# Recurrent states of a decayed attention: kept block-diagonal as they leave PSUM, in place of copies into zeroed tiles

## Chip, core and metric

One NeuronCore of a Trainium2 chip. The kernel is a single launch. The metric is the time of the slowest core in microseconds of the device, here of the only one. Lower is better.

## What is computed

The reference is a linear attention with decay, followed by two matmuls with a leaky activation between them. Inputs: q, k, v of (4 batches, 8 heads, 768 positions, 64), a decay `lam` per head, and weights `w_in` (512x2048), `w_out` (2048x512), `alpha` (2048).

```python
for b in range(nb):                      # blocks of 64 positions
    intra = einsum('bhic,bhjc->bhij', qb, kb) * Dmask
    intra = einsum('bhij,bhjd->bhid', intra, vb)
    inter = einsum('bhid,bhde->bhie', qb * lam_pow, kv_state)
    out[:, :, sl] = intra + inter
    kv_state = lam_block * kv_state + einsum('bhsd,bhse->bhde', kb * rev_pow, vb)
x = out.transpose(0, 2, 1, 3).reshape(3072, 512)
h = x @ w_in
return (maximum(h, 0) + alpha * minimum(h, 0)) @ w_out
```

The state `kv_state` is a 64x64 matrix for each batch and head. It carries everything that earlier blocks contribute to later ones.

## The kernel before

The kernel works with blocks of L = 128 positions, in pairs (W = 256), so there are three pairs of blocks, pb = 0, 1, 2, in each batch. A *unit* is one block pair of one batch and one half of the heads (four heads, `hh` = 0 or 1): 24 units, numbered in the list `units`. Two batches make a *column* c of 512 positions; six columns pass through the two weight matrices.

For each unit: q and k are cast to fp16 (`cast`), transposed on PE or by DMA (`transposes`, `transposed`), k is weighted with its decay (`key_decayed`), the transposed q too (`decayed`). `score_products` makes the scores with 64x64 tiles of PE, `masked` multiplies them with the decay mask on DVE. `state_products` (L432) makes the products of k and v with 64x64 tiles, one for each head, sixteen for each block. `inter` (L371) applies the states to the queries with full 128x128 matmuls that take two heads at once. So its weights must be a 128x128 matrix with the states of the two heads on the diagonal and zeros beside it.

Before the change there are two sets of tiles for the states. `R[b, hh, n]` holds the state behind block n - 1, dense: 128 partitions (two heads of 64), two head pairs, 64 columns. `RD[b, hh]` holds the two block-diagonal weights of the current pair. `zero_states` writes zeros into RD once on DVE; later only the diagonal is written. `states` (L459) does that. For the first pair (pb = 0) ACT copies the products of block 0 from PSUM into R (L486), and in two halves of 64 partitions into the diagonal of RD (L481); DVE adds the decayed state to the products of block 1 (`dense`, L469: one instruction for each head pair). For later pairs DVE runs `dense` for each block and POOL copies R into the diagonal of RD, four copies of 64 partitions for a unit (L495). The order of the two on ACT is set by the argument `first`.

`cluster(old, new)` (L497) puts two units together in one tile `acc` of two PSUM banks, one for each block: columns 0 to 255 of a bank hold the outputs of the old unit, 256 to 383 the state products of the new one. Every call takes a fresh tile from a pool with one buffer, so it begins when all that read the former tile are done. `state(n, pair)` (L518) makes the state products of a unit by themselves, in two other banks; it is called for units 1, 2, 3 and 6. `up` (L528) is the product with `w_in`, then ACT (L541) and DVE (L550) make the activation g; `down` and `down_last` are the product with `w_out`, and `store` brings the sums out through ACT. `fill` issues matmuls whose result nobody reads.

The order on every engine is written out by hand: a list of calls from L634 to L946 up to the third column, and behind it `attention_steps` and `weave`, which mix the steps of one column's attention with the matmuls of others. Each engine takes its instructions in the order of the calls and waits on semaphores. Loads of k, q and v are issued on SP, those of the weights on POOL (`load_win` L98, `load_wout` L110), and their places are in the same list. The start of the list, the calls for units 0 to 3, ends with the first `up`:

```python
cluster(None, 0, "A", "V")
...
state(1, "hh", "V")
...
cluster(0, None, "A")
...
cluster(1, None, "A")
state(2, "hh", "A")
...
cluster(2, None, "A")
scores(3)
...
state(3, "to", "A")
cluster(3, None, "V")
```

Of the kernel before, what the change touches and what calls it, by code (L numbers as in the profile page):

```python
# [11 lines left out]
def kernel(  # L12
# [52 lines left out]
    def load_alpha():  # L65
        nc.sync.dma_start(out=alpha_sb, in_=moe_alpha.rearrange("(t p) -> t p", p=128))

    R = {
        (b, hh, n): const.tile([128, 2, D], fp16, name=f"R{b}_{hh}_{n}")
        for b in range(B)  # L70
        for hh in range(2)
        for n in range(1, S // L)
    }
    RD = {
        (b, hh): const.tile([128, 2, 2, 2, D], fp16, name=f"RD{b}_{hh}")
        for b in range(B)
        for hh in range(2)
    }
# [3 lines left out]
    def load(c, bi, x, half=None):  # L82
# [6 lines left out]
        nc.sync.dma_start(  # L89
            out=raws[c, bi][i][:, heads, :],  # L90
            in_=(k, q, v)[i][b, heads, ds(pb * W, W), :].rearrange("h (p e) d -> p h (e d)", e=2),
        )
# [30 lines left out]
    def zero_states(batches, eng="V"):  # L123
        for b in batches:
            for hh in (1, 0):
                if eng == "G":
                    nc.gpsimd.memset(RD[b, hh].bitcast(int32), 0)
                else:
                    nc.vector.memset(RD[b, hh], 0.0)

    zero_states((1, 0))
# [25 lines left out]
    fill(4, "h", RD[1, 1].rearrange("p a e h d -> p (a e h d)"))  # L157
# [213 lines left out]
    def inter(n, ot):  # L371
        co, bo, ho = units[n]
        pbo, bb = co // 2, 2 * (co % 2) + bo
        for a in range(2):
            if 2 * pbo + a == 0:
                continue
            for hp in range(2):
                nc.tensor.matmul(  # L378
                    ot[a][:, hp, :].rearrange("p (e j) -> p e j", e=2),
                    lhsT=RD[bb, ho][:, a, hp].rearrange("p h d -> p (h d)"),  # L380
                    rhs=T[n]["qdT"][:, :, hp, ds(a * 64, 64)],
                    start=(hp == 0),
                    stop=False,
                    skip_group_check=True,
                )
# [26 lines left out]
    def intra(n, ot):  # L412
# [19 lines left out]
    def state_products(n, kv, fresh):  # L432
        t = T[n]
        for hp in range(2):
            for e in range(2):
                for hl in range(2):
                    for a in blocks_of(n):
                        p = ds(a * 64, 64)
                        nc.tensor.matmul(  # L439
                            kv[a][ds(hl * 64, 64), hp, :],  # L440
                            lhsT=t["kdec"][p, e, 2 * hp + hl, :],
                            rhs=t["v16"][p, 2 * hp + hl, e, :],
                            start=(fresh and hp == 0 and e == 0),
                            stop=(e == 1),
                            skip_group_check=True,
                        )

    def attended(n, acc, eng):
# [10 lines left out]
    def states(n, kv, first="A"):  # L459
# [18 lines left out]
        def diagonal():  # L478
            for hl in range(2):
                p = ds(hl * 64, 64)  # L480
                nc.scalar.activation(RD[b, hh][p, 1, :, hl, :], kv[0][p], AF.Copy)  # L481

        if pb == 0:
            if first == "A":
                diagonal()
            nc.scalar.activation(R[b, hh, 1], kv[0], AF.Copy)  # L486
            if first != "A":
                diagonal()
            dense()
            return  # L490
        dense()
        for a in range(2):
            for hl in range(2):
                p = ds(hl * 64, 64)
                nc.gpsimd.tensor_copy(out=RD[b, hh][p, a, :, hl, :], in_=R[b, hh, 2 * pb + a][p])  # L495

    def cluster(old, new, eng="A", first="A"):  # L497

        acc, ot, kv = accumulators()
        if old is not None:  # L500
            inter(old, ot)
        if new is not None:
            score_products(new)
        if old is not None:
            intra(old, ot)
        if new is not None:
            state_products(new, kv, old is None)
            masked(new)
        if old is not None:
            attended(old, acc, eng)  # L510
        if new is not None:
            states(new, kv, first)
# [5 lines left out]
    def state(n, pair, first="A"):  # L518
# [125 lines left out]
    zero_states((2,), "V")  # L644
# [30 lines left out]
    cluster(None, 0, "A", "V")  # L675
# [14 lines left out]
    state(1, "hh", "V")  # L690
# [11 lines left out]
    state(2, "hh", "A")  # L702
# [11 lines left out]
    state(3, "to", "A")  # L714
# [47 lines left out]
    zero_states((3,), "V")  # L762
    cast(7, "k16", "A")
    down(0, 0, 1, 4, "op")
    cluster(None, 4, "A", "V")
# [15 lines left out]
    cluster(5, 7, "A", "V")  # L781
# [27 lines left out]
    state(6, "hh", "A")  # L809
# [179 lines left out]
```

## Time and profile before

| what | value |
|---|---|
| median of 3 runs | 215.39 us (215.36 to 215.66) |
| the profiled execution | 215.25 us, its span 213.2 us |
| PE busy | 204.6 us (96%), 2084 matmuls |
| DVE busy | 135.4 us (64%) |
| ACT busy | 117.7 us (55%) |
| POOL busy | 79.8 us (37%) |
| chain that ended last | PE 91%, ACT 3%, DMA 2% |
| granted clock of PE | 0.998 |

The profile shows one execution. "Busy" is the share of time in which an engine has an instruction at work. PE is the matmul engine, DVE the vector engine, ACT the scalar engine, POOL the general one, SP only issues DMAs. Rows of a group give the line, engine, operation, output and inputs, shapes and count, then the busy time, the mean of one in ns, and the idle time before them with what ended it. Rows of the timeline give the start and the length in us. The chain of waits goes back from the last instruction to what released each step. The line numbers are those of the kernel before.

### The profile page before, as it was taken

The page shows a single profiled execution, that of the slowest core. Times are in us where ns is not written, and L with a number is a line of the kernel's source. Part 1 is how long each engine was busy: PE and PEld are TensorE (multiplying, and loading weights), DVE is VectorE, ACT ScalarE, POOL GpSimd, SP SyncE. Part 2 cuts the span into 40 slices and gives each one's busy share as a digit, 9 for nine tenths or more (in the row PEclk, how much of TensorE's full clock was granted, in tenths as well). Part 3 has the DMA queues.
Part 4 walks back from the last instruction along what each step waited for, and adds up shares of the span by engine and source line. Part 5 has one row for each costly group of instructions (what it writes and reads, how often), then busy time and mean ns, then how long its engine had stood idle before and what let it go on. Part 6 is the DMA issues. An engine that isn't in the chain of part 4 may idle for free.

```text
span 213.2 us, 5185 instructions
## 1 busy us (share of the span) xinstructions
PE 204.6 (96%) x2084; PEld 105.9 (50%) x2084; DVE 135.4 (64%) x247; ACT 117.7 (55%) x225; POOL 79.8 (37%) x148
## 2 busy tenths in 40 slices
PE   7677999999999999999999999999999999999994
PEld 2354444555545465455554554554554444444453
DVE  6795788767899877979965655555546344444000
ACT  7987766577685537366654644644534543444121
POOL 3597002425446664336688358348301000000000
PEclk9999999999999999999999999999999999999999
DMA  6999999998968599996929996044011001110212
GB/s 165 290 274 205 207 205 288 251 300 255 283 158 234 107 173 277 229 242 187 233 46 263 222 246 167 0 101 98 0 52 49 33 20 51 49 49 3 98 49 98
DMA packets 60603, 33.37 MB, mean 157 GB/s; under 512 B 16276, under 2 KB 57636, under 8 KB 60580
## 3 DMA queue, kind: packets, MB, share of 16 engines
q1 hardware_dynamic: 56340, 28.85, 55.3%
q0 software_dynamic: 4224, 4.19, 11.9%
q8 instruction: 16, 0.26, 0.5%
q14 instruction: 7, 0.06, 0.1%
q10 hardware_dynamic: 16, 0.00, 0.0%
HBM read 27.27 MB, written 6.29 MB: 157 GB/s over the span
## 4 chain that ended last, share of the span: by engine, by line
PE 91%; ACT 3%; DMA 2%; POOL 1%; DVE 1%; issue 0%; ACTq 0%; POOLq 0%
PE h_ps L533 39%; PE o_ps L563 33%; PE o_ps L586 7%; PE s L394 4%; PE acc L419 2%; DMA kraw<-in_k_dram 2%; PE acc L378 2%; PE acc L439 1%; PE tp L321 1%; POOL kdec L293 1%; ACT qkT L252 1%; ACT RD L481 1%; DVE sm L405 1%; PE unread L148 1%; ACT qk L252 1%; PE tpx L341 1%
## 5 line engine op out<-in xcount | busy, mean ns | idle before, releaser
L550 DVE SCALAR_TENSOR_TENSOR g<-m,oma,h_ps 128x512 f16<-128x512 f32 (+1 forms) x98 | 71.1, 736 | 50.2 <-ACT m L541 48.3
L533 PE MATMUL h_ps<-xT,w_in_sb 128*128 128x512 f16 (+1 forms) x392 | 92.9, 375 | 0.0
L541 ACT ACTIVATE m<-h_ps 128x512 f32<-128x512 f32 (+1 forms) x98 | 57.4, 588 | 56.6 <-PE h_ps L533 56.4
L563 PE MATMUL o_ps<-w_out_sb,g 128*128 128x512 f16 x320 | 80.2, 380 | 0.0
L533 PEld LDWEIGHTS <-w_in_sb 128*128 128x128 f16 x392 | 37.9, 98 | 43.1 <-issue 0.2
L563 PEld LDWEIGHTS <-g 128*128 128x128 f16 x320 | 29.8, 98 | 33.5
L495 POOL COPY RD<-R 64x128 f16<-64x128 f16 x64 | 19.7, 309 | 43.0 <-DVE R L469 39.5
L405 DVE TENSOR_TENSOR sm<-s,dmask 128x1024 f16<-128x1024 f32 x24 | 29.3, 1221 | 4.0 <-PE s L394 3.9
L576 ACT ACTIVATE o_sb<-o_ps 128x512 f32<-128x512 f32 (+2 forms) x26 | 14.7, 564 | 20.1 <-PE o_ps L586 10.9
L293 POOL TENSOR_TENSOR kdec<-kraw,kdecay 128x512 f16<-128x512 f32 x18 | 19.2, 1072 | 5.4 <-DMA kraw<-in_k_dram 5.0
L252 ACT ACTIVATE xT<-acc 128x512 f16<-128x512 f32 x22 | 13.1, 598 | 10.5 <-PE acc L439 8.8
L355 POOL TENSOR_TENSOR qdT<-qkT,qdecay 128x512 f16<-128x512 f16 (+1 forms) x15 | 15.5, 1036 | 2.9 <-ACT qdecay L237 2.2
L586 PE MATMUL o_ps<-w_out_sb,g 128*128 128x512 f16 (+2 forms) x96 | 14.1, 308 | 0.0
L469 DVE SCALAR_TENSOR_TENSOR R<-R,rdecay,acc 128x64 f16<-128x64 f16 x56 | 12.4, 276 | 0.9 <-ACT R L486 0.5
L256 POOL CAST qk<-kraw 128x512 f16<-128x512 f32 x14 | 8.5, 610 | 11.9 <-DMA kraw<-in_k_dram 6.8
L586 PEld LDWEIGHTS <-g 128*128 128x128 f16 x96 | 8.1, 98 | 6.1
L394 PE MATMUL s<-qkT 64*64 64x128 f16 x384 | 10.0, 221 | 0.9 <-DVE qkT L254 0.4
L256 POOL CAST v<-vraw 128x512 f16<-128x512 f32 x15 | 9.3, 621 | 3.4 <-DMA vraw<-in_v_dram 2.4
L252 ACT ACTIVATE qk<-qraw 128x512 f16<-128x512 f32 x17 | 10.4, 623 | 0.0
L419 PE MATMUL acc<-sm,v 64*64 64x128 f16 x384 | 9.6, 218 | 0.1
L378 PE MATMUL acc<-qdT,RD 128*128 128x128 f16 x80 | 8.4, 219 | 0.9 <-ACT RD L481 0.8
L378 PEld LDWEIGHTS <-RD 128*128 128x128 f16 x80 | 6.2, 98 | 6.0 <-ACT RD L481 1.1
(66 smaller groups left out, 116.8 us busy)
## 6 DMA issues: line engine op xcount, KB each, us to landing
out_dram<-o_sb SPq DMA_DIRECT2D x23, 256.0 KB, 2.3
kraw<-in_k_dram SPq DMA_DIRECT2D x18, 256.0 KB, 6.5
vraw<-in_v_dram SPq DMA_DIRECT2D x14, 256.0 KB, 5.7
qraw<-in_q_dram SPq DMA_DIRECT2D x7, 512.0 KB, 5.9
qraw<-in_q_dram SPq DMA_DIRECT2D x10, 256.0 KB, 5.4
vraw<-in_v_dram SPq DMA_DIRECT2D x5, 512.0 KB, 5.9
w_in_sb<-in_moe_w_in_dram POOLq DMA_DIRECT2D x4, 512.0 KB, 8.6
w_out_sb<-in_moe_w_out_dram POOLq DMA_DIRECT2D x4, 512.0 KB, 12.7
```

The costliest lines, as they stand in the source:

```text
L252: nc.scalar.activation(out, in_, AF.Copy)
L256: nc.gpsimd.tensor_copy(out=out, in_=in_)
L293: engine(eng).tensor_tensor(out=kdec, in0=kr, in1=kdecay[:, ds(4 * hh, 4), :].rearrange("p h e -> p e h").unsqueeze(3).to_broadcast([128, ...
L378: nc.tensor.matmul(ot[a][:, hp, :].rearrange("p (e j) -> p e j", e=2), lhsT=RD[bb, ho][:, a, hp].rearrange("p h d -> p (h d)"), rhs=T[n][" ...
L394: nc.tensor.matmul(t["s"][ds(a * 64, 64), hl, hp, 1 - e, :].rearrange("p (e j) -> p e j", e=2), lhsT=t["qkT"][p, 1, e, hp, ds(a * 64, 64)] ...
L405: nc.vector.tensor_tensor(out=t["sm"].rearrange("p a h x j -> p (a h) x j"), in0=t["s"].rearrange("p a h x j -> p (a h) x j"), in1=mask_of ...
L495: nc.gpsimd.tensor_copy(out=RD[b, hh][p, a, :, hl, :], in_=R[b, hh, 2 * pb + a][p])
L533: nc.tensor.matmul(h_ps[:, 0:n] if bi is None else h_ps[:, 0:n].rearrange("p (e j) -> p e j", e=2), lhsT=w_in_sb[:, gi, ts(f, 128)], rhs=x ...
L541: nc.scalar.activation(m[:, 0:n], h_ps[:, 0:n], AF.Relu, scale=-1.0)
L550: nc.vector.scalar_tensor_tensor(out=g, in0=mv, scalar=oma[:, f : f + 1], in1=hv, op0=ALU.mult, op1=ALU.add)
L563: nc.tensor.matmul(o_ps, lhsT=lhs(c, f, t), rhs=w_out_sb[:, f, :], start=(f == 0), stop=(f == NF - 1),)
L586: nc.tensor.matmul(o_ps[:, 0:n], lhsT=lhs(c, f, t), rhs=w_out_sb[:, f, ds(x, n)], start=(f == 0), stop=(f == NF - 1),)
```

## The change

RD, `zero_states`, the `diagonal` copies and POOL's copies go. R itself becomes block-diagonal: four tiles for each batch and head half (the fifth state takes the place of the first), each with two head pairs, two places for the head, and 64 columns, so that `inter` reads it as it is. The state products are written into the diagonal of 256 columns of a bank, where the columns beside the diagonal hold zeros. In `acc`, now one tile for the whole kernel, the zeros are written once by DVE at the start. In the banks of `state`, which other work uses in between, two 128x256 matmuls of zeros go ahead of the products, and the products then add to them. ACT's copy into R and DVE's `dense` take 256 and 128 columns for what were 128 and 64, zeros included. Seven calls of the list lose an argument, two calls of `zero_states` go; the list is else as it was.

```diff
-    RD = {(b, hh): const.tile([128, 2, 2, 2, D], fp16, name=f"RD{b}_{hh}") ...}
+    R = {}
+    for b in range(B):
+        for hh in range(2):
+            for n in range(1, S // L):
+                if n > 4:
+                    R[b, hh, n] = R[b, hh, n - 4]
+                    continue
+                R[b, hh, n] = const.tile([128, 2, 2, D], fp16, name=f"R{b}_{hh}_{n}")
...
-    zero_states((1, 0))
+    zeros = const.tile([128, CH], fp16, name="zeros")
+    nc.vector.memset(zeros, 0.0)
+    acc = ps.tile([128, 2, 512], fp32, tag="acc", name="acc")
+    nc.vector.memset(acc[:, :, 256:512], 0.0)
...
-    fill(4, "h", RD[1, 1].rearrange("p a e h d -> p (a e h d)"))
+    fill(4, "h", zeros)
...
-    def accumulators():
-        acc = ps.tile([128, 2, 512], fp32, tag="acc", name="acc")
-        ot = [acc[:, a, 0:256].rearrange("p (h i) -> p h i", h=2) for a in range(2)]
-        kv = [acc[:, a, 256:384].rearrange("p (h d) -> p h d", h=2) for a in range(2)]
-        return acc, ot, kv
+    ot = [acc[:, a, 0:256].rearrange("p (h i) -> p h i", h=2) for a in range(2)]
+    kv_acc = [acc[:, a, 256:512].rearrange("p (h l d) -> p h l d", h=2, l=2) for a in range(2)]
...
-                    lhsT=RD[bb, ho][:, a, hp].rearrange("p h d -> p (h d)"),
+                    lhsT=R[bb, ho, 2 * pbo + a][:, hp].rearrange("p l d -> p (l d)"),
...
-                            kv[a][ds(hl * 64, 64), hp, :],
+                            kv[a][ds(hl * 64, 64), hp, hl, :],
...
-        def diagonal():
-            for hl in range(2):
-                p = ds(hl * 64, 64)
-                nc.scalar.activation(RD[b, hh][p, 1, :, hl, :], kv[0][p], AF.Copy)
         if pb == 0:
-            if first == "A":
-                diagonal()
             nc.scalar.activation(R[b, hh, 1], kv[0], AF.Copy)
-            if first != "A":
-                diagonal()
-            dense()
-            return
         dense()
-        for a in range(2):
-            for hl in range(2):
-                p = ds(hl * 64, 64)
-                nc.gpsimd.tensor_copy(out=RD[b, hh][p, a, :, hl, :], in_=R[b, hh, 2 * pb + a][p])
...
     def state(n, pair):
         t = [bank_of(x, "kv") for x in (("h", "h") if pair == "hh" else ("tk", "op"))]
-        kv = [x[:, 0:128].rearrange("p (h d) -> p h d", h=2) for x in t]
-        state_products(n, kv, True)
-        states(n, kv, first)
+        for x in t:
+            nc.tensor.matmul(x[:, 0:256], lhsT=zeros[:, 0:128], rhs=zeros[:, 0:256], start=True, stop=False, skip_group_check=True)
+        kv = [x[:, 0:256].rearrange("p (h l d) -> p h l d", h=2, l=2) for x in t]
+        state_products(n, kv, False)
+        states(n, kv)
```

More of the change, by code (lines that the diff above doesn't have):

```diff
@@ L66, in load_alpha, with load @@
         nc.sync.dma_start(out=alpha_sb, in_=moe_alpha.rearrange("(t p) -> t p", p=128))
[L68 to L78, printed above, removed]
+    R = {}
[6 more added lines that the diff above has]
+                R[b, hh, n] = const.tile([128, 2, 2, D], fp16, name=f"R{b}_{hh}_{n}")
     raws = {}
-    def load(c, bi, x, half=None):
+    def load(c, bi, x, half=None, queue="S"):
         pb, b = c // 2, 2 * (c % 2) + bi
@@ L504, in cluster @@
         if old is not None:
-            intra(old, ot)
+            intra(old)
         if new is not None:
-            state_products(new, kv, old is None)
+            state_products(new, kv_acc, old is None)
             masked(new)
         if old is not None:
-            attended(old, acc, eng)
+            attended(old, eng)
         if new is not None:
-            states(new, kv, first)
+            states(new, kv_acc)
     def scores(n):
@@ L689 @@
     cast(2, "v16", "G")
-    state(1, "hh", "V")
+    state(1, "hh")
     load(1, 0, "q", 0)
@@ L701 @@
     cluster(1, None, "A")
-    state(2, "hh", "A")
+    state(2, "hh")
     query_decay(1, 0)
@@ L713 @@
     load(1, 0, "q", 1)
[L714 removed]
+    state(3, "to")
     cluster(3, None, "V")
@@ L808 @@
     load(3, 0, "k", 1)
-    state(6, "hh", "A")
+    state(6, "hh")
     decayed(8, "V")
```

32 lines of the change are left out of this document (11 added, 21 removed).

## The prediction

> **What bounds the kernel now.** I read the page's engine table and slices first, then the busy time by stage, then the chain of waits through the start, then the timeline of PE there.
>
> ```profile
> span 213.2 us, 5185 instructions
> PE   7677999999999999999999999999999999999994
> ```
> ```profile
> 0.00:20.48 20.48, 15.03 (x261) 8.56 (x262) 15.30 (x45) 17.40 (x43) 14.69 (x27) 1.00 1.05 235
> 20.48:56.00 35.52, 35.50 (x410) 18.95 (x409) 28.16 (x49) 23.52 (x48) 7.82 (x13) 1.00 1.13 254
> 56.00:106.00 50.00, 50.00 (x613) 26.41 (x611) 44.20 (x83) 30.70 (x55) 28.11 (x54) 1.00 0.96 207
> ```
> The columns of the second fence are stretch, length, then busy time (instructions) of PE, weight loads, DVE, ACT and POOL, clock, DMA. From 20.48 us PE is never idle. In the chain of waits (next fence, last row) four 128x512 matmuls take 0.86 there, 216 ns each, over and over; so after 20.48 the end moves only by work added to PE, by a wait that is new, or by an earlier start. Up to 20.48 PE is busy 15.03 of 20.48, ACT 17.40: the chain there runs mostly on ACT.
>
> ```profile
> 10.98 0.28 ACT R L486
> 11.26 0.15 ACT RD L481
> ...
> 11.72 0.63 ACT qk L252
> 12.35 0.53 ACT v L252
> ...
> 16.60 0.14 ACT RD L481
> ...
> 17.05 0.28 ACT R L486
> ...
> 18.15 0.45 PE s L394 x16
> 18.62 1.24 DVE sm L405
> 19.90 0.42 PE acc L419 x16
> ...
> 144.28 0.86 PE o_ps L563 x4
> ```
>
> The end of that chain is unit 3's copy qkT, which ACT begins behind RD, R and qdecay, its scores, their mask on DVE, and the products on the masked scores; then PE runs without a gap. The two halves of RD fill 11.26 to 11.70.
>
> **The change, part by part.** Rows of the groups by form:
>
> ```profile
> L495 POOL COPY RD<-R 64x128 f16<-64x128 f16 x64 | 19.7, 309 | 43.0 <-DVE R L469 39.5 <-ACT m L541 1.8
> L469 DVE SCALAR_TENSOR_TENSOR R<-R,rdecay,acc 128x64 f16<-128x64 f16 x56 | 12.4, 276 | 0.9 <-ACT R L486 0.5 <-ACT RD L481 0.4
> L129 DVE MEMSET RD<- 128x256 uint32 x8 | 2.2, 272 | 0.9 <-PEq L973 0.9
> L204 DVE SCALAR_TENSOR_TENSOR dmask<-rel_f,loglam,drop 128x192 f32<-128x192 f32 x8 | 2.8, 397 | 0.0
> L541 ACT ACTIVATE m<-h_ps 128x256 f32<-128x256 f32 x4 | 1.5, 381 | 1.3 <-PE h_ps L533 1.3
> L586 PE MATMUL o_ps<-w_out_sb,g 128*128 128x256 f16 x16 | 1.9, 272 | 0.0
> ```
>
> POOL loses its 64 copies RD<-R (19.7 us). They run after 56 us, under a full PE; their 43.0 us of waiting shows POOL had time. Worth 0. DVE loses eight memsets of 272 ns and gets one like them and one of 512 fp32 in PSUM, 0.54 us by the same rate; the first one still lets the warm-up matmuls begin, and the second ends before POOL's index tables that DVE needs next. 0 as well. No DMA and no place in a list moves.
>
> ACT, units 0 to 7: one 128x256 copy in place of R and two halves of RD. Before, 10.98 to 11.72, 0.74 us. After: 0.38 by the 128x256 row of L541, less the overlap with the next queued instruction, which the two rows below show as 0.10 (0.39 long, the next begins 0.29 behind it): 0.28. Each such unit gives ACT 0.46 us.
>
> ```profile
> 17.22 0.39 ACT L237 ACTIVATE qdecay<-pos_f,llp 128x128 f32<-128x128 f32 x1
> 17.51 0.59 ACT L252 ACTIVATE qkT<-tpx 128x512 f16<-128x512 f16 x1
> ```
>
> DVE: each of the 64 state updates (L469) has 128 elements, not 64. From 64 (276 ns) to 192 (397) is 0.95 ns an element: +0.06 each, +0.12 for a unit of the first or last block pair, +0.25 for one of the middle pair.
>
> PE: each of four `state` calls gets two 128x256 products of zeros. In full stream 2 x 0.108 = 0.216 (half of 216 ns each). Inside 64x64 work they also change the array's form twice; the next rows give that price.
>
> ```profile
> 12.11 0.42 PE L394 MATMUL s<-qkT 64*64 64x128 f16 x16 [0.21 <-DVE sm L405]
> 12.92 0.32 PE L439 MATMUL kv<-v,kdec 64*64 64x64 f16 x16 [0.40 <-ACT v L252]
> 13.17 0.40 PE L341 MATMUL tpx<-ident,qk 128*128 128x128 f16 x4
> 13.41 0.28 PE L378 MATMUL acc<-qdT,RD 128*128 128x128 f16 x2
> 13.61 0.42 PE L419 MATMUL acc<-sm,v 64*64 64x128 f16 x16
> 13.96 0.40 PE L341 MATMUL tpx<-ident,qk 128*128 128x128 f16 x4
> ...
> 15.36 0.42 PE L419 MATMUL acc<-sm,v 64*64 64x128 f16 x16
> 15.61 0.29 PE L439 MATMUL kv<-v,kdec 64*64 64x64 f16 x16
> 16.17 0.38 PE L341 MATMUL tpx<-ident,qk 128*128 128x128 f16 x4 [0.26 <-ACT qkT L252]
> 16.39 1.24 PE L148 MATMUL unread<-ident 128*128 128x512 f16 x5
> ```
>
> Sixteen 64x128 products take 0.25 up to more 64x64 work (15.36 to 15.61) and 0.35 up to full-array work (13.61 to 13.96): 0.10 to change. Two full products of 0.054 take 0.20 up to 64x64 work (13.41 to 13.61): 0.09 to change back. A pair between 64x64 groups costs 0.10 + 0.216 + 0.09 = 0.41.
>
> Now the start, step by step. Unit 1: ACT's v ends 0.46 earlier (12.42); the scores of 12.11 leave PE at 12.46, zeros and change put kv at 12.77 instead of 12.92: -0.15, so the transposes end at 13.42 and their copy on ACT begins at 13.46 instead of 14.03 (-0.57: the 0.15 and the two RD copies' time). Scores of unit 2, the xT copy and the products behind it follow at -0.57: 15.36 becomes 14.79. There 0.35, zeros 0.216 and 0.09 put kv at 15.45 (-0.16), the transposes at 15.70, the five filler matmuls at 15.92 (-0.47) and, 1.28 later as before, the next products at 17.20. Unit 3's copy qkT is by then ready (ACT: R at 15.89, qdecay 16.17, qkT 16.46 to 17.06, for 17.51), so the scores no longer wait for it and go 0.25 behind the products: 17.45 instead of 18.15, -0.70. The mask follows at 17.92, the products on it at 19.20 instead of 19.90. Two other inputs of that point: unit 3's state (zeros, kv at 18.11, R to 18.83, against RD before) and POOL's qdT, not moved and done at 18.65, let the inter-block products run from 18.88, 0.32 ahead of the mask. The dense run starts at 19.78: **-0.70**. Its weights allow that:
>
> ```profile
> 17.96 0.69 POOL L355 TENSOR_TENSOR qdT<-qkT,qdecay 128x256 f16<-128x256 f16 x1
> ```
> ```profile
> L98 POOL DMA_DIRECT2D w_in_sb<-in_moe_w_in_dram x4: 757/774/925, 12.3 to 16.5; - x4
> DMA to landing us min/median/max: 6.9/8.6/10.4
> ```
>
> The first of four is issued at 12.3 and has the shortest way, 6.9: landed at 19.2.
>
> Behind the start: `state(6)` adds its pair in full stream, **+0.22**. DVE's longer updates meet PE in the middle block pair:
>
> ```profile
> 75.81 1.23 DVE L405 TENSOR_TENSOR sm<-s,dmask 128x1024 f16<-128x1024 f32 x1 [0.75 <-PE s L394]
> 76.95 0.85 DVE L469 SCALAR_TENSOR_TENSOR R<-R,rdecay,acc 128x64 f16<-128x64 f16 x4
> 77.71 1.38 DVE L355 TENSOR_TENSOR qdT<-qkT,qdecay 128x512 f16<-128x512 f16 x2
> ```
> ```profile
> 78.64 0.39 PE L378 MATMUL acc<-qdT,RD 128*128 128x128 f16 x4
> ```
>
> The first qdT of that pair ends at 78.40 (77.71 and half of 1.38); with 0.25 more PE gets it about 0.06 late: **+0.06**. Elsewhere I take the cover to be thicker, and price that as a rival. Sum: -0.70 + 0.22 + 0.06 = **-0.42 us**. The profiled execution took 215.25 (span 213.2 and 2.05 around it), 0.14 under the median of 215.39; the sum gives 214.83 for it and 214.97, taken as **214.95**, for the median. Bounds: a pair at the start costs between 0 (PE idles there) and twice its 0.41; the start gains between 0 and what w_in's landing allows, 19.25 instead of 20.48, 1.23.
>
> A rule speaks against my price of a change of form. The Trainium skill, "TensorEngine Tiling (Array Packing)", section Tiling Modes, says that a change of tiling mode drains TensorE. By "TensorE: Matmul & The Clock Gate", section Single matmul latency, a warm 256-column matmul takes (398 + 256)/2.4 = 272 ns. The trace agrees with both figures (272 in the L586 row, and a change costs time), but it shows 0.20 for two 128-column products and the change, not the 0.27 that a whole drain would make of it.
>
> **The rivals.** (1) A full drain: 64x64 work begins only when the last zero product has run its whole 272 ns, 0.07 later in each pair than I take. Two pairs lie on the way to the scores: the start gains 0.56, the sum is -0.28, 215.10. Against it stands the 0.20 of 13.41 to 13.61. By the Trainium skill's drain rule this is the time; the trace bears it out in part. (2) The pairs vanish in PE's waits (0.40 idle before 12.92, 0.26 before 16.17): each start step takes ACT's 0.46, the dense run starts when w_in has landed, 215.39 - 1.2 + 0.28 = 214.5. (3) The start does not move, as w_in lands later than 20.4 or another input is late: 215.39 + 0.28 = 215.67. Against: the load's place is not moved. (4) Slower: DVE becomes the bound between 56 and 106 us, where it is busy 44.20 of 50.00. The 32 updates there add 32 x 0.06 = 2.0 us. It decides from the point where more than 0.9 us of this reaches PE (0.48 of gain and 0.43 for the bound); with half of it the time is 215.39 - 0.48 + 1.0 = 215.9, with all 216.9. For it: the thin cover at 78.64. Against: DVE waits 0.75 us for PE at 75.81, so it catches up between such groups.
>
> **How the numbers follow.** A measurement of this kernel tells about 0.2%, 0.43 us, from no change. My forecast, 214.75 to 215.2 by itself, lies on that bound: 0.46, two thirds of it faster. Rival 1: 0.10, same. Rival 2: 0.11, faster. Rival 3: 0.11, same. Rival 4: 0.22, slower. So faster 0.42, same 0.36, slower 0.22. The range 214.4 to 216.0 takes in rivals 1 to 3 and the lower half of 4.
>
> **What would show it.** Right: the first h_ps matmul near 19.8; one ACT copy of about 0.38 where three stood; state updates near 0.34; the pair of zeros at about 51.5 us in stream, PE busy without a gap behind the start. Wrong: the first h_ps after 20.2, scores of unit 3 that still wait, updates above 0.40, or PE waits named DVE R, g or qdT between 56 and 106 us.

## The result and the profile after

The changed kernel takes 214.52 us in the median of 20 runs (214.39 to 216.15); the kernel before, on the same chips, 215.33 (215.11 to 215.77). The ratio is 0.9974, 95% interval 0.9962 to 0.9985: 0.26% faster, with no change just outside the interval. The two medians lie further apart, 0.81 us or 0.38%, because the slower ones of the 20 runs count in the ratio too. The profiled execution took 214.56 us against 215.25. Its span, to two more places, is 212.78 against 213.18. So 0.40 us of the 0.69 lie inside the span, and 0.29 outside it: 1.78 us around it where there were 2.07.

Two more things differ. The runs spread more: 8 of the 20 lie more than 0.3 us above the lowest, against 3 of 20 before. And PE, not ACT, now carries the chain through most of the start.

The page of the changed kernel, its head and the engine table's first row:

```profile
span 212.8 us, 5116 instructions
...
PE 206.7 (97%) x2092; PEld 106.5 (50%) x2092; DVE 138.2 (65%) x241; ACT 114.8 (54%) x209; POOL 60.2 (28%) x84
```

Busy time by stage (same columns as in the prediction's fence), cut at the first h_ps matmul:

```profile
0.00:19.88 19.88, 16.84 (x267) 9.07 (x267) 15.16 (x41) 15.81 (x35) 14.44 (x27) 1.00 1.04 236
19.88:56.00 36.12, 36.12 (x414) 19.38 (x413) 28.89 (x48) 22.74 (x41) 8.41 (x13) 1.00 1.15 256
56.00:106.00 50.00, 50.00 (x611) 26.35 (x610) 45.40 (x81) 30.38 (x55) 19.06 (x25) 1.00 0.92 208
```

The dense run of PE begins at 19.88 in place of 20.48. From there to the end of the span it takes 192.90 us, 0.20 more than before (213.18 less 20.48). DVE is 1.2 us busier between 56 and 106 us, and PE still shows no idle time there in this view.

The groups by form (busy us, mean ns of one):

```profile
L458 DVE SCALAR_TENSOR_TENSOR R<-R,rdecay,acc 128x128 f16<-128x128 f16 x56 | 16.1, 342 | 0.1
...
L495 PE MATMUL kv<-zeros 128*128 128x256 f16 x8 | 1.6, 277 | 0.0
L468 ACT ACTIVATE R<-kv 128x256 f16<-128x256 f32 x4 | 1.6, 389 | 0.9 <-PE kv L428 0.9
L468 ACT ACTIVATE R<-acc 128x256 f16<-128x256 f32 x4 | 1.5, 381 | 1.0 <-PE acc L428 0.9
```

PE's timeline through the start (start, length):

```profile
12.14 0.42 PE L383 MATMUL s<-qkT 64*64 64x128 f16 x16 [0.21 <-DVE sm L394]
12.49 0.39 PE L495 MATMUL kv<-zeros 128*128 128x256 f16 x2
12.81 0.32 PE L428 MATMUL kv<-v,kdec 64*64 64x64 f16 x16
...
17.27 0.42 PE L408 MATMUL acc<-sm,v 64*64 64x128 f16 x16
17.52 0.46 PE L383 MATMUL s<-qkT 64*64 64x128 f16 x16
17.92 0.39 PE L495 MATMUL kv<-zeros 128*128 128x256 f16 x2
```
```profile
19.05 0.28 PE L367 MATMUL acc<-qdT,R 128*128 128x128 f16 x2 [0.49 <-ACT R L468]
19.30 0.42 PE L408 MATMUL acc<-sm,v 64*64 64x128 f16 x16
19.65 0.39 PE L140 MATMUL unread<-ident 128*128 128x512 f16 x1
```

A pair of zeros stands between the scores and the state products of a unit, 0.32 us from its start to theirs. Unit 3's scores follow the products at 17.27 without a wait, and the last wait of the start is now unit 3's R copy on ACT.

### The profile page after: what moved, and what is told of

It is laid out like the page before. It is cut to its first block, busy times and chain, and to the rows that moved or that the text cites. A ratio compares the mean times of both kernels' runs of the same rounds, so it can differ in the third digit from the quotient of the medians.

```text
span 212.8 us, 5116 instructions
## 1 busy us (share of the span) xinstructions
PE 206.7 (97%) x2092; PEld 106.5 (50%) x2092; DVE 138.2 (65%) x241; ACT 114.8 (54%) x209; POOL 60.2 (28%) x84
## 4 chain that ended last, share of the span: by engine, by line
PE 96%; DVE 2%; ACT 1%; issue 0%; ACTq 0%; DVEq 0%
PE h_ps L508 39%; PE o_ps L538 33%; PE o_ps L561 7%; PE s L383 4%; PE acc L408 3%; PE unread L140 3%; PE acc L367 2%; PE tp L313 1%; PE acc L428 1%; PE tpx L333 1%; PE unread L138 1%; DVE sm L394 1%; DVE qkT L246 1%; PE kv L495 0%; PE kv L428 0%; DVE dmask L196 0%
## 5 line engine op out<-in xcount | busy, mean ns | idle before, releaser
L347 POOL TENSOR_TENSOR qdT<-qkT,qdecay 128x512 f16<-128x512 f16 (+1 forms) x15 | 15.2, 1013 | 17.1 <-DMA qkT<-qk 8.1
L458 DVE SCALAR_TENSOR_TENSOR R<-R,rdecay,acc 128x128 f16<-128x128 f16 x56 | 16.1, 342 | 0.1
L367 PEld LDWEIGHTS <-R 128*128 128x128 f16 x80 | 6.2, 98 | 5.6 <-ACT R L468 0.6
L367 PE MATMUL acc<-qdT,R 128*128 128x128 f16 x80 | 8.4, 219 | 0.5 <-ACT R L468 0.5
L383 PEld LDWEIGHTS <-qkT 64*64 64x64 f16 x384 | 6.5, 106 | 3.7 <-issue 1.4
```

What stands on the lines that cost most here:

```text
L367: nc.tensor.matmul(ot[a][:, hp, :].rearrange("p (e j) -> p e j", e=2), lhsT=R[bb, ho, 2 * pbo + a][:, hp].rearrange("p l d -> p (l d)"), r ...
L383: nc.tensor.matmul(t["s"][ds(a * 64, 64), hl, hp, 1 - e, :].rearrange("p (e j) -> p e j", e=2), lhsT=t["qkT"][p, 1, e, hp, ds(a * 64, 64)] ...
L458: nc.vector.scalar_tensor_tensor(out=R[b, hh, m + 1][:, hp], in0=R[b, hh, m][:, hp], scalar=rdecay[:, 2 * hh + hp : 2 * hh + hp + 1], in1= ...
```

## The experiments

Each ratio is to the kernel before, with its 95% interval. "Outside" is the time of a run less its span.

| kernel | median (lowest to highest), runs | ratio | outside |
|---|---|---|---|
| changed kernel | 214.52 (214.39 to 216.15), 20 | 0.9974 (0.9962 to 0.9985) | 1.74 to 1.84 |
| 1 ACT copies ahead of R | 216.84 (216.78 to 217.07), 5 | 1.0074 (1.0062 to 1.0086) | 1.74 to 1.81 |
| 2 POOL copies | 215.05 (215.03 to 215.29), 11 | 0.9990 (0.9982 to 0.9999) | 2.19 to 2.29 |
| 3 narrow zeros | 214.44 (214.25 to 215.52), 12 | 0.9974 (0.9962 to 0.9986) | 1.75 to 1.83 |
| 4 k early | 214.56 (214.43 to 214.88), 5 | 0.9964 (0.9951 to 0.9977) | 1.73 to 1.78 |
| 5 64 memsets, POOL | 215.13 (214.93 to 216.33), 10 | 1.0000 (0.9986 to 1.0014) | 1.74 to 1.84 |
| 6 64 memsets, DVE | 214.66 (214.41 to 216.51), 10 | 0.9984 (0.9966 to 1.0002) | 1.75 to 1.82 |
| 7 ACT copies behind R | 216.03 (216.03 to 216.06), 4 | 1.0033 (1.0020 to 1.0046) | 1.76 to 1.84 |
| 8 start rearranged | 215.41 (214.19 to 269.96), 12 | 1.0000 (0.9973 to 1.0026) | 1.74 to 1.86 |
| 9 cast later | 214.62 (214.48 to 214.75), 5 | 0.9966 (0.9954 to 0.9978) | 1.73 to 1.82 |
| 10 narrow, cast later | 214.38 (214.36 to 215.19), 7 | 0.9966 (0.9953 to 0.9978) | 1.76 to 1.83 |
| 11 and filler moved | 214.38 (214.38 to 214.81), 5 | 0.9964 (0.9952 to 0.9977) | 1.76 to 1.81 |
| 12 narrow, cast later, k early | 214.51 (214.44 to 214.85), 6 | 0.9967 (0.9955 to 0.9979) | 1.74 to 1.85 |

### 1 and 7: ACT's copies put back

```diff
 # 1: ahead of the R copy in the units where the kernel before has them so; 7: behind it in all
+        def spare():
+            for hl in range(2):
+                p = ds(hl * 64, 64)
+                nc.scalar.activation(spare_rd[p, 1, :, hl, :], kv[0][p, :, hl, :], AF.Copy)
         if pb == 0:
             nc.scalar.activation(R[b, hh, 1], kv[0], AF.Copy)
+            spare()
         dense()
```

> The changed kernel with ACT's two 64x128 copies per unit of the first position block put back, at the places where the kernel before has them, but into a tile that nothing reads. The output is untouched. Theory (the start got earlier because ACT lost two copies of about 0.23 us in each unit): unit 3's R copy stands behind 0.46 us of copies again and the earlier units' copies push it too, so the first h_ps product moves from 19.88 to between 20.3 and 20.8 and the time goes up by 0.5 to 0.9 us, to 215.0 to 215.4. Rival (ACT's copies were hidden, the start moved for another reason, and the zero pairs or PE set it now): first h_ps within 0.1 us of 19.88, time within 0.2 us of the changed kernel's 214.5.

> The changed kernel with ACT's two 64x128 copies per unit put back behind the R copy in every unit, into a tile that nothing reads, so that the R copy itself does not wait for its own unit's copies (with them ahead, where the kernel before has them for some units, the first h_ps product was at 21.5 us and the time 216.84). The output is untouched. Theory A (what the start gained came from work gone from ACT's queue, wherever it stood): units 1 and 2 still push unit 3's R copy by 0.4 to 0.9 us; first h_ps at 20.3 to 20.8, time 214.9 to 215.4. Theory B (what counted was only what stands ahead of the copy that PE waits for): first h_ps within 0.2 us of 19.88, time 214.4 to 214.7.

Both came out slower than either theory gave: 2.3 and 1.5 us above the changed kernel. With the copies behind R (PE's timeline of that kernel):

```profile
13.22 0.32 PE L429 MATMUL kv<-v,kdec 64*64 64x64 f16 x16 [0.19 <-ACT v L245]
...
15.09 0.42 PE L384 MATMUL s<-qkT 64*64 64x128 f16 x16 [0.43 <-DVE R L459]
...
18.82 0.42 PE L384 MATMUL s<-qkT 64*64 64x128 f16 x16 [0.18 <-ACT qkT L245]
...
21.15 1.03 PE L515 MATMUL h_ps<-xT,w_in_sb 128*128 128x256 f16 x6
```

Against the changed kernel, unit 1's scores are 0.15 us late (12.29 for 12.14), and this lateness is there from PE's transposes at 7.2 us, ahead of all copies. Unit 1's state products are 0.41 late (13.22 for 12.81), unit 2's scores 0.91 (15.09 for 14.18), unit 3's 1.30 (18.82 for 17.52). So the copies add 0.26, 0.50 and 0.39 in these three steps; the dense run starts 1.27 late. ACT's timeline behind unit 0's R copy, first in the changed kernel, then in the seventh:

```profile
11.01 0.38 ACT L468 ACTIVATE R<-acc 128x256 f16<-128x256 f32 x1
11.29 0.62 ACT L244 ACTIVATE qk<-qraw 128x512 f16<-128x512 f32 x1
```
```profile
11.16 0.38 ACT L474 ACTIVATE R<-acc 128x256 f16<-128x256 f32 x1
11.44 0.56 ACT L471 ACTIVATE spare_rd<-acc 64x128 f16<-64x128 f32 x2
12.02 0.63 ACT L245 ACTIVATE qk<-qraw 128x512 f16<-128x512 f32 x1
```

From R to the next work it is 0.28 in the changed kernel, 0.86 in the seventh, and 0.74 in the kernel before (10.98 to 11.72), whose R copy was narrower. So the copies put back take 0.58 of ACT for a unit, 0.12 more than the change gave it. Theory A stands: what counts is work gone from ACT's queue, wherever it stood. Its size was too low, because it counted two units and not three, and none of units 4 to 7, whose copies add 0.30 at the inter-block products of 44.37 us (0.05 is won back at 39.1). Theory B is out. Ahead of R the copies cost their time once more, since the inter-block products of unit 3 then wait for R behind them (in the first kernel until 20.69, and PE's wait there is 1.11 us).

The first kernel has the copies where the kernel before has them. So it is, but for POOL's copies and the unread target, the kernel before with the rest of the change added: the wider R copy, the pairs of zeros and DVE's longer updates. Its span is 214.97 us, 1.79 more than that of the kernel before. The changed kernel's span is 2.19 below it: that is what ACT's sixteen copies cost at these places, against 1.49 behind R (214.27 in the seventh kernel). So the 0.40 of gain in the span is a small difference of two larger effects.

### 2, 5 and 6: POOL's copies, and what lies outside the span

```diff
 # 2, in states()
+        if pb > 0:
+            for a in range(2):
+                for hl in range(2):
+                    p = ds(hl * 64, 64)
+                    nc.gpsimd.tensor_copy(out=spare_rd[p, a, :, hl, :], in_=R[b, hh, 2 * pb + a][p, :, hl, :])
 # 5, ahead of down_last; 6 the same with nc.vector
+    for _ in range(64):
+        nc.gpsimd.memset(spare, 0.0)
```

> The changed kernel with POOL's four 64x128 copies per unit of the later position blocks put back, reading the state and writing a tile that nothing reads. The output is untouched. Theory (these copies were hidden inside the span): the span stays within 0.15 us of 212.7 to 212.8. On the part of the time that lies outside the span (2.07 us in the kernel before, 1.76 to 1.79 in the changed kernel) two rivals: if it hangs on the length of POOL's program, it goes back to about 2.05 and the time up by about 0.3 to 214.8; if it does not, it stays at 1.76 to 1.79 and the time stays at 214.5. A third rival, that POOL's reads stretch DVE's work and DVE has no slack left in the stretch from 56 to 106 us: span up by 0.3 or more, with waits of PE on DVE's products in that stretch.

> The changed kernel with 64 memsets of one element per partition added at the end of POOL's program, into a tile that nothing reads. The output is untouched. Theory (the time outside the span follows the length of POOL's program: 1.77 us with 84 instructions of POOL in the profile, 2.07 and 2.24 with 148): span 212.7 to 212.8 as before, outside it 2.05 to 2.25, so the time is 214.8 to 215.05. Rival (the outside part followed something else, the state copies themselves or their place in the program): 1.77 outside and 214.5.

> The changed kernel with the same 64 small memsets at the end of DVE's program in place of POOL's, where DVE has nothing else left to do. The output is untouched. If the time outside the span follows POOL's program alone: 1.77 outside, time 214.5. If it follows the length of any engine's program, or of all together (5185 instructions in the kernel before, 5116 in the changed one): 2.05 or more outside, time 214.8 or more.

With POOL's copies back, the span is 212.93, 0.16 longer, and 0.11 of it arises at the inter-block products of 78.23 us, which wait for DVE's qdT: the one they wait for took 0.79 us in place of 0.69, beside POOL's copies (the mean of the six 128x512 ones is 955 ns, without the copies 683). The rest of the time, 0.43 to 0.45, is outside the span. The theory of the fifth and sixth kernels is that the length of POOL's program makes it. The fifth kernel seemed to refute it, for outside stayed at 1.74 to 1.84; but its span grew by 0.4 while PE's last product started 0.07 earlier than in the changed kernel. Its memsets run from 150 to 160 us, so they hold up nothing at the end by their own work. Counting from that last start to the end of the run puts all in one row: 5.07 us in the changed kernel (214.56 less 209.49), 5.52 with POOL's copies (215.15 less 209.63), 5.53 with POOL's memsets (214.94 less 209.41), 5.07 with DVE's (215.85 less 210.78), and 5.37 in the kernel before (215.25 less 209.88). So 64 more instructions of POOL, copies or memsets, cost 0.30 to 0.46 at the very end; 64 of DVE cost nothing there. (In the other kernels it is 5.06 to 5.10, and 5.19 to 5.20 in the three that load unit 5's k on POOL's queue.) The DMA queues between 200 and 216 us (packets, MB, share) show one difference, first in the kernel before, then with POOL's memsets, then in the changed kernel:

```profile
q1 hardware_dynamic: 864, 1.05, 17.6%
q14 instruction: 1, 0.01, 0.2%
```
```profile
q1 hardware_dynamic: 864, 1.05, 17.9%
q14 instruction: 1, 0.01, 0.2%
```
```profile
q1 hardware_dynamic: 864, 1.05, 17.6%
```

One more block of instructions is fetched after the last output where POOL's program is long (with POOL's copies too), and none where it is short. In the trace that packet starts 1.4 us behind the span's end in the kernel before, 1.0 with the copies and 0.3 with the memsets. DVE's memsets bring a packet too, but at 202.9 us, before the last products. That the end waits for this packet is not shown, and one trace speaks against it: with the memsets the span's end is 3.74 us behind the start of the last product, where it is 3.29 in the changed kernel and the kernel before, so the delay is over before the packet starts. Shown is the cost of a longer POOL program; its mechanism is open.

### 3: zeros only beside the diagonal, by 64x64 tiles

```diff
-        for x in t:
-            nc.tensor.matmul(x[:, 0:256], lhsT=zeros[:, 0:128], rhs=zeros[:, 0:256], start=True, ...)
+        for hl in range(2):
+            for a in range(2):
+                p = ds(a * 64, 64)
+                nc.tensor.matmul(kv[a][ds(hl * 64, 64), :, 1 - hl, :], lhsT=zeros[p, 0:64],
+                    rhs=zeros[p, 0:128].rearrange("p (h d) -> p h d", h=2), start=True, stop=False, ...)
```

> The changed kernel with the two 128x256 zero products of each standing state product replaced by four products of 64x64 tiles that write zeros only beside the diagonal, two heads at a time, so that PE does not change its tile size. The output is the same. Theory (a pair costs 0.3 to 0.4 us at the start because of its columns and the change of tile size, and the start chain runs over it): a set of four narrow ones costs about 0.12, the first h_ps product moves from 19.88 to 19.4 to 19.7, the pair ahead of unit 6's products in the full stream gets about 0.1 cheaper, and the time falls by 0.3 to 0.6 us, to 213.9 to 214.2. Rival (the chain's last links are ACT's R copy, the decay ahead of it on ACT, and DVE's mask, which do not follow PE): first h_ps at 19.8 or later, time down by 0.1 us at most. A limit for both: the last w_in slice lands at about 19.2.

Two stretches of PE's timeline in this kernel:

```profile
12.28 0.42 PE L383 MATMUL s<-qkT 64*64 64x128 f16 x16 [0.21 <-DVE sm L394]
12.50 0.25 PE L498 MATMUL kv<-zeros 64*64 64x128 f16 x4
12.62 0.32 PE L428 MATMUL kv<-v,kdec 64*64 64x64 f16 x16
...
19.00 0.27 PE L367 MATMUL acc<-qdT,R 128*128 128x128 f16 x2 [0.80 <-POOL qdT L347]
19.34 0.42 PE L408 MATMUL acc<-sm,v 64*64 64x128 f16 x16
```

From the scores to the state products it is 0.34 in place of 0.67: the price of the pair was as the theory has it. But the gain stops at unit 3, where PE waits 0.80 us for POOL's qdT and then for DVE's mask; the dense run starts at 19.91. The rival is right on the start. (The limit of 19.2 is the landing of the first w_in slice, which the first `up` reads, not of the last, which landed at 27.0 in the changed kernel.) In the full stream the narrow ones save 0.16 us at unit 6's state, and the lowest run is 0.14 below that of the changed kernel.

### 4, 9, 10 and 12: the spread

```diff
 # 4: unit 5's k, second half of the heads, on POOL's queue ahead of the third w_out slice
+    load(1, 0, "k", 1, "G")
     load_wout(2)
...
-    load(1, 0, "k", 1)
 # 9: DVE's cast of unit 3's v behind unit 2's mask (10: 9 and 3; 12: 9, 3 and 4)
-    cast(3, "v16", "V")
     cast(2, "v16", "G")
...
     scores(2)
+    cast(3, "v16", "V")
```

> The changed kernel with the load of unit 5's k (second half of the heads) moved from the SP queue, where it lands at 38.52 us just as PE wants it, to the POOL queue ahead of the third w_out slice. The output is the same. Theory (loads that land just in time in the stretch from 36 to 50 us now decide there, and their spread from run to run makes the slower eighth to third of the changed kernel's runs, 214.8 to 216.2): the idle of PE ahead of unit 5's transposes goes, the median falls by 0.1 us, and runs above 214.7 are fewer than 1 in 8. Rival 1 (the spread comes from somewhere else): as many runs above 214.7 as the changed kernel has, 8 of 20, median within 0.1 us. Rival 2 (the third w_out slice or the other loads get late in its place): time up by 0.2 us or more.

> The changed kernel with DVE's cast of unit 3's v moved behind unit 2's mask, so that it no longer starts within 0.04 us of POOL's cast of unit 2's v. The output is the same. In the profiled run with the 64 small DVE memsets this cast took 1.97 us instead of 0.42, ended with POOL's cast and decayed keys, held unit 1's state update and with it PE for 1.1 us, and that run came out at 215.85. Theory (this meeting of the two casts, 0.02 us apart in the changed kernel and 0.16 in the kernel before, makes the changed kernel's runs above 214.7, 8 of 20): with it gone at most 1 run in 10 lies above 0.3 us over the lowest, the lowest stays at 214.3 to 214.5 and so does the median. Rival (the spread has other causes): as before about 4 runs in 10 lie above.

> The narrow zeros of the third experiment and the later cast of v together, the output the same. Theory (the two are independent: 0.1 us from the zeros, the spread from the cast): lowest and median at 214.25 to 214.4, at most 1 run in 10 above 0.3 us over the lowest. Rival (the narrow zeros bring nothing once the spread is gone, the start being set by POOL's decayed queries and DVE's mask): median as with the later cast alone, within 0.05 us.

> Three edits together, the output the same: the narrow zeros, the later cast of unit 3's v, and the early load of unit 5's k on the POOL queue. In the profiled run of the first two together (215.19) PE waited 0.6 us at 39 us for unit 5's k, in the profiled run with 64 small DVE memsets it waited 1.1 us for the stretched cast; these are the two places that a traced slow run has shown. Theory (these two make the spread of the changed kernel): lowest 214.3 to 214.4, median within 0.1 us of it, no run above 0.3 us over the lowest. Rival (other places remain): a quarter or more of the runs above 0.3 us over the lowest; the trace of such a run, if it is the profiled one, names the next wait.

Two of the longer runs happened to be the profiled ones, and each shows a cause. The first is that of DVE's memsets (215.85); the timelines of PE, DVE and POOL:

```profile
16.71 0.28 PE L496 MATMUL kv<-zeros 128*128 128x256 f16 x1 [1.06 <-DVE R L459]
```

```profile
14.18 1.97 DVE L247 CAST v<-vraw 128x512 f16<-128x512 f32 x1
16.06 0.59 DVE L459 SCALAR_TENSOR_TENSOR R<-R,rdecay,kv 128x128 f16<-128x128 f16 x2
```
```profile
14.22 0.62 POOL L249 CAST v<-vraw 128x512 f16<-128x512 f32 x1
14.79 1.05 POOL L286 TENSOR_TENSOR kdec<-kraw,kdecay 128x512 f16<-128x512 f32 x1
```

The next two fences show the same instructions in the changed kernel:

```profile
13.98 0.42 DVE L246 CAST v<-vraw 128x512 f16<-128x512 f32 x1
```
```profile
14.00 0.87 POOL L248 CAST v<-vraw 128x512 f16<-128x512 f32 x1
14.84 1.04 POOL L285 TENSOR_TENSOR kdec<-kraw,kdecay 128x512 f16<-128x512 f32 x1
```

The two casts begin 0.02 to 0.04 us apart. In the changed kernel's profile DVE's takes its 0.42 and POOL's is stretched to 0.87; in the longer run POOL's takes 0.62, DVE's 1.97, past the end of POOL's next instruction, and a zero product of unit 2 waits 1.06 us for the bank that DVE's update has not read. The Trainium skill, "SBUF — State Buffer", section Who interferes with whom, has the rule: a DVE cast in a two-port mode and an instruction of GpSimd (POOL) exclude each other, and whichever is issued first holds the ports for its whole length. The longer run's trace agrees on the exclusion; but here the loser stood through two instructions of POOL, and the recorded starts do not tell which wins: in eight other traces, the changed kernel's among them, DVE's cast begins 0.01 to 0.04 us ahead of POOL's and takes its 0.42, and in the longer run it begins ahead too.

The second is that of narrow zeros with the cast moved (215.19). Its waits of PE:

```profile
PE tp L313 <- DVE qk L246: 0.6, 1, 0.6
```

At 39 us unit 5's transposes wait for DVE's cast of k, which ran at 39.20 in place of 38.54 because its load landed later.

With the cast moved, none of five runs lies more than 0.3 us above the lowest (largest 0.27); with the early k, one of five (0.45); with the cast moved and the narrow zeros, two of seven (0.83); with all three, one of six (0.41); in the eleventh kernel, which has the moved cast and the narrow zeros, one of five (0.43). With the narrow zeros alone it is five of twelve (1.27). But the second kernel (11 runs) and the first and seventh (9) have the casts as close and show none, so the counts do not settle how much of the spread these two causes make. What makes the 0.4 that remains is open.

### 8 and 11: a faster start tried

```diff
 # 8, with 3 and 4
-    load_wout(1)
-    fill(5, "tk")
+    fill(2, "tk")
...
     decayed(3, "G")
-    query_decay(0, 0)
+    load_wout(1)
...
     cluster(3, None, "V")
+    query_decay(0, 0)
...
-    fill(1, "h")
 # 11, with 3 and 9: all five fill matmuls kept, behind state(3) (bank "h"); fill(1) kept
```

> An attempt at a faster version with the same output: the narrow zeros and the early load of unit 5's k together, and at the start the links that then decided removed: the filler of five products ahead of unit 2's products cut to two and the single one ahead of the first h_ps product left out, the query decay that stands ahead of unit 3's R copy on ACT moved behind it, and the second w_out slice's issue on POOL moved behind unit 3's decayed queries. Theory (the start is a chain over ACT's R copy, POOL's decayed queries and DVE's mask, which the filler holds back by up to 0.6 us): first h_ps at 19.25 to 19.5, bounded by the last w_in slice at about 19.2, and the time at 213.8 to 214.1. Rival (the loads, not PE, set the pace of the stretch from 30 to 50 us, so an earlier start is lost again there): first h_ps at 19.25 to 19.5, but the unit products after 38 us at the same times as in the changed kernel, time 214.3 to 214.5. On the spread: if late loads of unit 5's k make it, no more than 1 run in 8 lies above 0.3 us over the lowest.

> The same, and at the start the same amount of filler as the changed kernel has, but behind unit 3's state products in place of ahead of unit 2's products; the query decay that stands ahead of unit 3's R copy on ACT moved behind it, and the second w_out slice's issue on POOL behind unit 3's decayed queries. The output is the same. Theory (the filler held the chain back; its amount, not its place, kept the granted clock at 1.0, which had fallen to 0.984 to 0.998 in most runs when it was cut): first h_ps at 19.4 to 19.7, clock 1.0, median 213.9 to 214.1. Rival A (the clock falls whenever dense PE work starts earlier): first h_ps as early, but runs at clocks under 0.995 and times of 215 and more. Rival B (the loads pace the stretch after it): first h_ps as early, unit products after 38 us where the changed kernel has them, 214.3 to 214.5.

Neither start came below 19.75. In the eighth, with less filler, the granted clock fell. Its busy time by stage (columns as above, the clock third from the end):

```profile
16.00:21.40 5.40, 4.12 (x80) 2.30 (x79) 3.46 (x8) 2.62 (x7) 5.00 (x7) 0.83 1.24 205
21.40:27.00 5.60, 5.60 (x26) 2.69 (x25) 3.49 (x6) 3.55 (x7) 0.00 (x0) 0.86 1.24 207
```

In the changed kernel it is 1.00 in both stretches. Over the runs of the eighth the mean clock went from 1.00 down to 0.984, with times up to 217.23, and in one to 0.758, which took 269.96 and is left out of the ratio. With the same amount of filler at another place, the eleventh, it was 0.998 or 1.00 in every run, and the median 214.38: the gain that the theory expected did not come, as rival B has it, but the first h_ps was not early either (19.94), so it was not the loads. That the filler's amount, not its place, kept the clock fits both kernels; they differ in the early k and the cast too, so it is not shown by itself. Rival A was not put to the test, since the dense work did not start earlier.

What held the start is shown by PE's timeline of the eleventh and the twelfth kernel:

```profile
17.11 0.36 PE L383 MATMUL s<-qkT 64*64 64x128 f16 x11
17.69 0.27 PE L383 MATMUL s<-qkT 64*64 64x128 f16 x5 [0.22 <-issue]
```
```profile
17.22 0.28 PE L383 MATMUL s<-qkT 64*64 64x128 f16 x6
17.68 0.36 PE L383 MATMUL s<-qkT 64*64 64x128 f16 x10 [0.19 <-issue]
```

PE stops in the middle of unit 3's scores and waits for nothing that the profile shows ("issue"). Counted in the programs (weight loads and products, from 0), it stops ahead of the same instruction of PE, number 448, in the eighth, tenth, eleventh and twelfth kernels, whichever of the scores that is, after gaps of 0.35 to 0.50 us, and goes on at 17.69 to 17.70. In the changed kernel, the second, the third, the fifth and the ninth this instruction starts between 17.67 and 17.69 too, with gaps of 0.05 to 0.15 ahead of it; in the others, where PE comes there later (17.76 to 19.0 us), there is none. So a supply of PE's instructions, not any engine's work, seems to set 17.69. The Trainium skill, "Runtime: NRT & Kernel Launch", section Instruction fetch mechanics, says that sequencers fetch blocks of 16 KiB, 256 instructions, and that this is mostly hidden. The traces agree on the size: a queue for instructions moves sixteen packets (next row, of the changed kernel's page: packets, MB, share), the first of them at 15.2 us, and PE runs 4184 weight loads and products, 16.3 such blocks. That one of them is what PE waits for was not tested; the first packet took 1.2 us in the changed kernel, so it was in 1.3 us before the instruction started, and what fills that time is not known.

```profile
q8 instruction: 16, 0.26, 0.5%
```

None of the versions around 0.9965 is told apart from another; the tenth and eleventh have the lowest median, 214.38, 0.14 below the changed kernel's.

## Why the prediction was right, and where it was not

The likeliest case came in: faster, by the start, with one pair of zeros given back behind it. The time itself is below the 214.75 to 215.2 of that case: the median fell by 0.81 us where 0.44 was forecast. Most of the difference is time outside the span, for which the sum had no term. The terms one by one:

- **ACT gives 0.46 us per unit.** Right for ACT's queue: 0.74 from R to the next work before, 0.28 after. Put back, the copies took 0.58 of ACT and delayed PE by 0.26, 0.50 and 0.39 (seventh kernel).
- **A pair costs 0.41 inside 64x64 work.** Right: 0.67 from the scores to the state products, less the 0.25 of the scores alone. From the pair's start to the state products it is 0.32; I took 0.31 and the full drain of rival 1 would have given 0.38.
- **The start moves by -0.70.** It moved by -0.60. Of the missing 0.10, 0.03 was there at unit 1's scores (12.14 for the 12.11 of the kernel before) and 0.07 at unit 3's, which began at 17.52, not 17.45. They then took 0.40 up to the next work, not 0.35: the gap of 0.05 at instruction 448, which the working did not have. So the mask's products ran at 19.30, not 19.20. ACT's R copy, which I had ready at 18.83, ended at 18.99:

```profile
18.24 0.39 ACT L229 ACTIVATE qdecay<-pos_f,llp 128x128 f32<-128x128 f32 x1
18.61 0.38 ACT L468 ACTIVATE R<-kv 128x256 f16<-128x256 f32 x1
```

  It began 0.05 behind the end of unit 3's state products on PE (18.24 and 0.32), as unit 1's did (13.18 behind 13.13). By the 0.29 that a qdecay takes up to ACT's next work it could have begun at 18.53. So it is late mainly because the state products ran at 18.24, not 18.11. POOL's qdT, taken as not moved, ended at 18.81, not 18.65, but ahead of R. The two inputs, 0.32 apart in the working, are 0.25 apart (19.05 and 19.30).
- **state(6) adds 0.22.** Right: PE's products are 0.22 later from there on (51.6 us). That the whole time behind the start grew by 0.20 is the sum of this and of three other steps, of which the working had one.
- **DVE's +0.06 at 78.64.** Right: it is 0.09, too short for the list of PE's waits. The last products ahead of the inter-block products, and these, before and after:

```profile
77.99 0.81 PE L563 MATMUL o_ps<-w_out_sb,g 128*128 128x512 f16 x3
78.64 0.27 PE L378 MATMUL acc<-qdT,RD 128*128 128x128 f16 x2
```
```profile
77.71 0.59 PE L538 MATMUL o_ps<-w_out_sb,g 128*128 128x512 f16 x2
78.23 0.29 PE L367 MATMUL acc<-qdT,R 128*128 128x128 f16 x2
```

  Before, the inter-block products follow three of 0.216 at once (0.65). After, two take 0.43, to 78.14, and PE goes on at 78.23, 0.06 behind the end of DVE's qdT (78.17). The updates take 342 ns, as worked out (276 + 60), and DVE is busy 45.40 of 50. By the starts of PE's products this is the only place behind 56 us that got later, so rival 4 did not come.
- **Units 4 to 7, taken as nothing.** The working stopped counting ACT's copies at unit 3. In the kernel before, PE waits 0.18 ahead of unit 5's inter-block products (45.09); in the changed kernel it does not (44.37), and with the copies put back behind R it waits 0.30 there. This -0.18 was not in the sum. Nor was a wait of 0.06 for unit 5's k at 39.1 us, which the kernel before does not have.
- **POOL's copies: 0, DVE's memsets: 0.** The memsets are: the warm-up matmuls start at 1.19 as before. For POOL's copies this is the term that was wrong. Inside the span they hid but for 0.11 to 0.16 us, by the second kernel; outside it the kernel before spent 0.29 more, the second kernel 0.43 to 0.45, and the sum had no term there.
- **Sum.** -0.42 for the span against -0.40 measured, by errors that nearly cancel: 0.10 at the start, 0.03 at DVE's wait and 0.06 at unit 5's k on one side, 0.18 at unit 5's inter-block products on the other. The 0.43 between 214.95 and 214.52 is 0.29 from the time outside the span and 0.06 from the kernel before, which runs at 215.33 in the larger sample; the rest is within the spread of the runs.

Rival 1 (a full drain, -0.56 at the start) is nearer to the measured -0.60 than my -0.70, but not by its mechanism: a pair took 0.32 up to the state products, not 0.38. Rival 2 (start at the landing of w_in, 214.5) gave nearly the measured time by a mechanism that did not happen: the first h_ps is 0.56 us later than that landing (19.32), and the pairs cost what they were priced at. Rival 3 fell with the start. So the direction and the main cause were foreseen; that the sum for the span came so close, and that the time fell inside the range, owe something to errors that cancel.

## What to carry to other kernels

Removing hidden instructions can still pay at the program's end, so compare the time outside the span as well as the span, and count from the last product to the end of the run when the two shift against each other. Where a chain runs over one engine's queue, price every instruction in that queue, not only those that someone waits for: copies that nothing reads, put back into ACT's queue, cost the start 0.26 to 0.50 us a unit. And when the links of a chain have been freed in turn without moving its end, look for the same instruction starting at the same time in every trace.

## What the runs showed of the hardware

- 64 more instructions on POOL cost 0.30 to 0.46 us behind the last product. An instruction packet is fetched there too, but that it makes the cost is not shown. 64 on DVE cost nothing at that place.
- A DVE cast of 0.42 us took 1.97 in one traced run when it began within 0.04 us of a POOL cast; in other traces as close, POOL's cast took 0.85 to 0.87 for 0.62 instead.
- PE stalled up to 0.50 us (17.19 to 17.69, in the eighth kernel) ahead of its instruction 448, which started at 17.67 to 17.70 in nine traces. The cause is open.
- With four of the start's filler matmuls cut, the granted clock fell to 0.83 and 0.86 from 16 to 27 us in the traced run; with the full amount at another place it was 0.998 to 1.00 over each run.
- Two 128x256 products of zeros between 64x64 groups cost 0.42 us, four 64x64 ones of 128 columns 0.09 (0.34 less the 0.25).
